# Score tiles computed once, and zero matmuls in the steps of a transformer kernel that have no side work

## The chip, the cores and the metric

The kernel runs on one core of a Trainium2 chip. Its engines work side by side and wait for each other by semaphores: TensorE (PE; its weight loads are shown apart as PEld) multiplies matrices into PSUM, ScalarE (ACT) and VectorE (DVE) read PSUM and write SBUF, GpSimd (POOL) does small things and issues some DMAs, SyncE (SP) issues the other DMAs. The metric is the device time of one execution in microseconds, the median of several.

## The reference

Two layers, each an attention block and a token mixer, over 2048 tokens of width 640, with 32 heads of width 20. Matrix inputs are bf16.

```python
def _A_ref(x, wqkv, wo):                       # x: [1, 2048, 640], H = 32, Dh = 20
    q, k, v = split_heads(x @ wqkv)
    scores = jnp.einsum("bhqd,bhkd->bhqk", q, k) * (Dh ** -0.5)
    p = _softmax(scores, axis=-1)
    o = jnp.einsum("bhqk,bhkd->bhqd", p, v)
    return merge_heads(o) @ wo

def _B_ref(x, w1, b1, w2, b2):                 # mixes along the 2048 tokens, F = 1536
    h = _layernorm(x, axis=-1)
    u = _gelu(jnp.einsum("bsd,sf->bdf", h, w1) + b1)
    y = jnp.einsum("bdf,fs->bds", u, w2) + b2
    return y.transpose(0, 2, 1)

x = x + _A_ref(_layernorm(x), A_wqkv, A_wo)    # twice, with the same weights
x = x + _B_ref(_layernorm(x), B_w1, B_b1, B_w2, B_b2)
```

The softmax is over 2048 x 2048 scores per head, so each attention takes 134 million exponentials.

## The kernel before

**Stages.** A start (layer norm, transposition, V and the first K and Q projections), attention 0, the mixer's two matmul stages with the next layer's start folded into the second, attention 1, the mixer again. The change lies inside `attention`, which runs twice, and in the constants made at the kernel's beginning.

**Units, chunks and tiles.** An attention has 4 query blocks of 512, 8 groups of 4 heads and 16 key tiles of 128, which is 512 units `(qb, g, kt)` in this order. Each unit has four chunks, one a head, of 128 keys x 512 queries, in the order of `HORDER = (0, 2, 1, 3)`. Chunks are taken three at a time, so that one score tile `S` has 128 x 1536 numbers in three PSUM banks; there are 683 tiles per attention (the last has two chunks) and two buffers for them. A score matmul (`s_matmul`, L320) uses 64 rows of the array; heads 0 and 1 of a group lie in the lower 64 rows and heads 2 and 3 in the upper 64, and two neighbours are told apart by a masked copy of the queries (`qev`, `qod`). `HORDER` alternates between the halves.

**A step.** The loop over `t` at the end of `attention` writes out, for each step: the scores of tile `t + 1` (`emit_S`), the exponential of tile `t` on ScalarE into a bf16 tile `P` (`emit_exp`, L348), the PV matmuls of a unit if the exponentials they need are at least one step old (`emit_PV`, L546), and fill (`emit_fills`). PV has four matmuls per unit, one a head, each with 32 columns (20 of V, one of ones that sums the denominators, padding), placed at the columns 0, 32, 64 and 96 of the array, all into the four quarters of one accumulator tile `acc`. It stays open over the 16 key tiles of a group; `start` is set at the first, and after the last `normalize` takes it out of `acc_tiles` and VectorE transposes and divides it (L357 to L364). There is one buffer for it. As 4 chunks make a unit and 3 a tile, three steps of four have a PV and one has none.

**Fill.** Other TensorE work is cut into groups in `fill_queue`: the K and Q projections of later groups and query blocks (L227), the output projection (L448, L481), and the first part of the mixer's first matmul (L421), whose sums go through `ustg` to DRAM by POOL's DMA queue. `emit_fills` takes up to `FILL_NOPV = 3.0` units of cost in a step without PV and `FILL_PV = 1.5` in one with, and pauses one step after each finished group. `planned_fill` says ahead of a step if it will have fill.

**The repeat.** In a step without fill, `emit_S` is given `reps = R_DEFAULT = 1` and writes the same score matmuls of tile `t + 1` a second time. The results are the same.

**Order.** All TensorE instructions are chained in the order in which they are written out (`pe`). The order of the other engines' instructions is found by a scheduler from the dependences. On POOL the kernel's beginning has the identity's memset (masks.py), `warm` (L98, L99), two bias loads (L118, L119, issued as DMAs) and the layer norm's `rstd` (L169); SP issues the loads of x (L776, L786) and of the weights.

Of the kernel before, what the change touches and what calls it, by code (L numbers as in the profile page):

```python
# [11 lines left out]
BF16 = mybir.dt.bfloat16  # L12
# [12 lines left out]
VW = 24  # L25

CFG = dict(
    R_DEFAULT=1,
    FILL_NOPV=3.0,
    FILL_PV=1.5,  # L30
    PV_LAGT=1,
# [8 lines left out]
def kernel(  # L40
# [12 lines left out]
    nc = tc.nc  # L53
# [11 lines left out]
    def pe(inst):  # L65
        tc.chain_iter_dep("pe_order", inst.ins)
        return inst
# [12 lines left out]
    consts = ctx.enter_context(tc.tile_pool(name="consts", bufs=1))  # L80
# [16 lines left out]
    warm = consts.tile([128, 1], F32, name="warm")  # L97
    nc.gpsimd.tensor_tensor(out=warm[:], in0=mhalf[:], in1=mhalf[:], op=ALU.mult)  # L98
    nc.gpsimd.tensor_tensor(out=warm[:], in0=warm[:], in1=mhalf[:], op=ALU.pow)  # L99
    x1lp = ctx.enter_context(tc.tile_pool(name="x1lp", bufs=1))  # L100
    x1last = x1lp.tile([128, 4, D], F32, name="x1last")
    hhp = ctx.enter_context(tc.tile_pool(name="hhp", bufs=1))
# [141 lines left out]
    def attention(st, x_in_ap, x_mid, uacc_l):  # L244
        layer = st.layer
        KT, hT = st.KT, st.hT
        with ExitStack() as p1:
# [18 lines left out]
            S_tiles, P_tiles, acc_tiles, qm_tiles, attnT_tiles = {}, {}, {}, {}, {}  # L266
# [21 lines left out]
            def on_unit_start(n):  # L288
                qb_n, g_n, kt_n = units[n]
                fill_state["unit"] = n  # L290
                if qb_n == 0 and kt_n == 0:
                    if g_n + KQA < NG:
                        enqueue_kq_for_group(g_n + KQA)
                    if g_n == max(0, NG - KQA) and NQB > 1:
                        enqueue_qproj(1)
                if qb_n >= 1 and g_n == 0 and kt_n == 2 and qb_n + 1 < NQB:
                    enqueue_qproj(qb_n + 1)
                if not proj_enqueue_done[0]:
                    last_k_block = max(0, NG - 1 - KQA)
                    if NQB == 1:  # L300
                        done = (qb_n == 0 and g_n >= last_k_block)
                    elif NQB == 2:
                        done = (qb_n == 0 and g_n >= max(0, NG - KQA)) or qb_n >= 1
                    else:
                        done = (qb_n == NQB - 2 and (g_n > 0 or kt_n >= 2)) or qb_n > NQB - 2
                    proj_enqueue_done[0] = done
                check_hT_dead()
                if kt_n == 0:
                    ensure_ready(qb_n, g_n)
                    prep_block(qb_n, g_n)  # L310
                if kt_n == NKT // 2 and n + NKT < NU:
                    nqb, ng, _ = units[n + NKT - kt_n]
                    if ("Q", nqb, ng) not in pending_keys():
                        prep_block(nqb, ng)

            def s_matmul(St, slot, n, j):
                qb, g, kt = units[n]
                jj = j // 2
                q = qm_tiles[(qb, g)][j % 2]
                pe(nc.tensor.matmul(St[:, slot, :], lhsT=KT[64 * jj:64 * jj + 64, g, kt * 128:(kt + 1) * 128],  # L320
                                    rhs=q[64 * jj:64 * jj + 64, :], start=True, stop=True,
                                    tile_position=(64 * jj, 0)))

            def emit_S(t, reps):
                cs = chunks[3 * t:3 * t + 3]
                for (n, j) in cs:
                    if j == HORDER[0]:
                        on_unit_start(n)
                St = sps.tile([128, 3, 512], F32, name="S")
                S_tiles[t] = St  # L330
                for _rep in range(reps + 1):
                    i = 0
                    while i < len(cs):
                        n, j = cs[i]
                        if i + 1 < len(cs) and cs[i + 1][0] == n and (j, cs[i + 1][1]) in ((0, 2), (1, 3)):
                            s_matmul(St, i, n, j)
                            s_matmul(St, i + 1, n, cs[i + 1][1])
                            i += 2
                        else:
                            s_matmul(St, i, n, j)  # L340
                            i += 1

            def emit_exp(t):
                St = S_tiles.pop(t)
                ncs = len(chunks[3 * t:3 * t + 3])
                P = ptp.tile([128, 3, 512], BF16, name="P")
                P_tiles[t] = P
                nc.scalar.activation(out=P[:, 0:ncs, :].rearrange("p a b -> p (a b)"),  # L348
                                     in_=St[:, 0:ncs, :].rearrange("p a b -> p (a b)"),
                                     func=ACT.Exp, scale=SCALE)  # L350
# [186 lines left out]
            def emit_PV(n):  # L537
                qb, g, kt = units[n]
                if kt == 0:
                    acc_tiles[(qb, g)] = accp.tile([128, 512], F32, name="acc")  # L540
                acc = acc_tiles[(qb, g)]
                for j in range(4):
                    ci = 4 * n + HORDER.index(j)
                    P = P_tiles[ci // 3]
                    hh = 4 * g + j
                    pe(nc.tensor.matmul(acc[32 * j:32 * j + 32, :],  # L546
                                        lhsT=Vaug[:, (kt * H + hh) * VW:(kt * H + hh) * VW + 32],
                                        rhs=P[:, ci % 3, :], start=(kt == 0), stop=(kt == NKT - 1),
                                        tile_position=(0, 32 * j)))
                for t_ in list(P_tiles.keys()):  # L550
                    if (3 * t_ + 2) // 4 <= n:
                        del P_tiles[t_]
                if kt == NKT - 1:
                    normalize(qb, g, acc_tiles.pop((qb, g)))
                    if qb == LASTQB and PARTIAL_LAST:
                        if g % 2 == 1:
                            enqueue_outproj_partial(qb, g)
                    elif g == NG - 1:
                        enqueue_outproj(qb)

            def emit_fills(budget, pool_alloc):
                fs = fill_state
                if fs["cooldown"] > 0:
                    fs["cooldown"] -= 1
                    return 0.0
                spent = 0.0
                while spent < budget:
                    if fs["cur"] is None:
                        if not fill_queue:
                            break  # L570
                        if fill_queue[0].get("not_before", 0) > fs["unit"] and budget < 100:
                            break
                        fs["cur"] = fill_queue.popleft()
                        fs["idx"] = 0
                        fs["tile"] = pool_alloc()
                    grp = fs["cur"]
                    grp["mms"][fs["idx"]](fs["tile"])
                    spent += grp["cost"][fs["idx"]]
                    fs["idx"] += 1
                    if fs["idx"] == len(grp["mms"]):  # L580
                        grp["evac"](fs["tile"])
                        fs["cur"] = None
                        fs["cooldown"] = CFG["FILL_GAP"]
                        break
                return spent
# [4 lines left out]
            def planned_fill():  # L590
                if fill_state["cooldown"] != 0:
                    return False
                if fill_state["cur"] is not None:
                    return True
                return len(fill_queue) > 0 and fill_queue[0].get("not_before", 0) <= fill_state["unit"]

            LAGT = CFG["PV_LAGT"]
            pv_done = 0
            emit_S(0, 0)
            for t in range(NTILES):  # L600
                has_fill = planned_fill()
                reps = 0 if has_fill else CFG["R_DEFAULT"]
                if t + 1 < NTILES:
                    emit_S(t + 1, reps)
                emit_exp(t)
                n_pv = 0
                while pv_done < NU and (4 * pv_done + 3) // 3 <= t - LAGT:
                    emit_PV(pv_done)
                    pv_done += 1
                    n_pv += 1  # L610
                emit_fills(CFG["FILL_PV"] if n_pv else CFG["FILL_NOPV"], misc_alloc)
            in_attention[0] = False
            while pv_done < NU:
# [149 lines left out]
    with ExitStack() as a_stack:  # L763
        st0 = open_a_scope(0, a_stack)
        with ExitStack() as p0:
# [29 lines left out]
            setup_wo()  # L795
            setup_biases()
        attention(st0, A_x[0], xd[0], uacc[0])
    with ExitStack() as a_stack:
        st1 = open_a_scope(1, a_stack)
# [59 lines left out]
```

## Time and profile before

| | |
|---|---|
| median of 3 runs | 2105.06 us (2104.55 to 2106.12) |
| the profiled execution's own time | 2106.7 us |
| its span | 2104.9 us |
| TensorE busy | 1953.5 us, 93%, 13278 matmuls |
| ScalarE busy | 1931.5 us, 92%, 1504 instructions |
| VectorE busy | 570.0 us, 27% |
| POOL busy | 148.2 us, 7% |
| exponentials (L348) | 1366, 1839.9 us busy, 1500 ns mean |
| score matmuls (L320) | 6014 |
| PV matmuls (L546) | 4096 |

How it is read: one execution is recorded by the profiler. Busy time counts an engine's own instructions; the mean of one can be longer than its share, since neighbours overlap. A group's row gives, after the counts, the busy time, the mean of one in ns, and the idle time of the engine just before these instructions with what ended most of it. The chain of waits is the work that ended last, followed back from the end: from each piece to what released it. The timeline merges neighbouring instructions of one kind (x8: eight of them); its first number is the start and its second the time that they took, in us, and a bracket gives the idle time before. A row of the windows view gives, for a stretch of time, its length and the busy time and count of PE, PEld, DVE, ACT and POOL, then the granted clock of TensorE (1.00 is full), the share of the DMA engines, and GB/s.

### The profile page before, as it was taken

The numbers are of one execution on the slowest core, as the hardware profiler recorded it, in microseconds if no ns is written. First come the engines' busy times: TensorE is split into PE (matmuls) and PEld (weight loads), VectorE is DVE, ScalarE is ACT, GpSimd is POOL, SyncE is SP. The second block draws the span as 40 slices with busy tenths as digits, with TensorE's granted clock in tenths as the row PEclk, the third lists the DMA queues.
The fourth block names the chain that finished last, engine by engine and source line by source line (L and its number), as shares of the span: only waits on it lengthen the run. The fifth ranks groups of instructions, "written<-read, shape, count | busy, mean of one in ns | idle before, by whom it ended". The sixth has DMA issues, their size and how long they took to land.

```text
span 2104.9 us, 31825 instructions
## 1 busy us (share of the span) xinstructions
PE 1953.5 (93%) x13278; PEld 657.3 (31%) x13278; DVE 570.0 (27%) x1231; ACT 1931.5 (92%) x1504; POOL 148.2 (7%) x218
## 2 busy tenths in 40 slices
PE   7999999999999999997999999999999999999979
PEld 4222222233223332223542222222332233222335
DVE  6122222221322132223642122322113220322242
ACT  5999999999999999996349999999999999999952
POOL 2000000110012001110000000001100120011000
PEclk9999999999999999998999999999999999999989
DMA  5000000110034012223620000001101340222245
GB/s 129 1 1 1 1 18 22 61 53 10 29 58 71 1 35 44 37 26 118 211 81 1 1 1 1 26 28 65 47 14 38 66 63 1 57 49 36 38 121 182
DMA packets 90737, 96.88 MB, mean 46 GB/s; under 512 B 9696, under 2 KB 68192, under 8 KB 90592
## 3 DMA queue, kind: packets, MB, share of 16 engines
q1 hardware_dynamic: 70464, 71.22, 11.0%
q0 software_dynamic: 20128, 23.62, 7.5%
q8 instruction: 104, 1.70, 0.3%
q14 instruction: 41, 0.34, 0.1%
HBM read 55.48 MB, written 39.32 MB: 45 GB/s over the span
## 4 chain that ended last, share of the span: by engine, by line
ACT 58%; PE 25%; issue 13%; DVE 3%; DMA 1%; POOL 0%; SPq 0%; DVEq 0%; ACTq 0%; POOLq 0%
ACT P L348 58%; PE S L320 10%; PE y L741 4%; PE acc L546 3%; PE misc L227 3%; PE pp L218 2%; PE big L670 1%; PE misc L448 1%; DMA ua<-uacc 1%; PE pp L227 0%; DVE T L357 0%; PE S L481 0%; DMA x0in<-in_A_x_dram 0%; DVE bnst L158 0%; PE misc L481 0%
## 5 line engine op out<-in xcount | busy, mean ns | idle before, releaser
L348 ACT ACTIVATE P<-S 128x1536 bf16<-128x1536 f32 (+1 forms) x1366 | 1839.9, 1500 | 8.3 <-PE S L320 7.0
L320 PE MATMUL S<-qev,KT 64*128 64x512 bf16 x2962 | 836.8, 377 | 96.2 <-ACT P L348 90.1
L320 PE MATMUL S<-qod,KT 64*128 64x512 bf16 x3052 | 838.2, 379 | 9.1 <-ACT P L348 4.6
L320 PEld LDWEIGHTS <-KT 64*128 64x128 bf16 x6014 | 326.7, 93 | 655.5 <-issue 486.4
L546 PE MATMUL acc<-P,Vaug 128*32 128x512 bf16 x4096 | 409.9, 389 | 6.2 <-DVE T L357 4.3
L546 PEld LDWEIGHTS <-Vaug 128*32 128x32 bf16 x4096 | 106.5, 92 | 439.0 <-issue 439.0
L427 DVE COPY ustg<-misc 128x512 f32<-128x512 f32 (+1 forms) x144 | 70.0, 486 | 296.6 <-PE misc L421 296.5
L169 POOL TENSOR_TENSOR rstd<-veps,mhalf 128x1 f32<-128x1 f32 x64 | 35.5, 554 | 1187.6 <-DVE veps L164 1068.4
L432 POOL DMA_DIRECT2D uacc<-ustg x96 | 83.0, 864 | 473.6 <-DVE ustg L427 444.3
L421 PE MATMUL misc<-h2st,w1st 128*128 128x512 bf16 (+1 forms) x576 | 115.8, 303 | 0.0
L741 PE MATMUL y<-uT,w2s 128*128 128x512 bf16 (+1 forms) x768 | 107.8, 299 | 3.4 <-ACT uT L684 3.4
L508 DVE CAST QTq<-misc 128x512 bf16<-128x512 f32 x62 | 42.8, 691 | 214.2 <-PE misc L227 214.2
L227 PE MATMUL misc<-hh,wq_pad 128*128 128x512 bf16 x310 | 98.9, 385 | 0.0
L357 DVE STREAM_TRANSPOSE T<-acc 128x512 f32<-128x512 f32 x64 | 45.9, 717 | 186.4 <-PE acc L546 186.4
L508 DVE CAST KT<-misc 128x512 bf16<-128x512 f32 x56 | 38.7, 691 | 212.9 <-PE misc L227 212.9
L227 PE MATMUL misc<-hh,wk_pad 128*128 128x512 bf16 x280 | 87.2, 385 | 0.0
L279 DVE TENSOR_SCALAR qev<-QTq,mask_ev 128x512 bf16<-128x512 bf16 x64 | 22.6, 353 | 235.4 <-PE S L320 234.8
L448 PE MATMUL misc<-wo_pad,attnT 128*128 128x512 bf16 (+1 forms) x384 | 76.8, 303 | 0.0
L741 PEld LDWEIGHTS <-w2s 128*128 128x128 bf16 x768 | 59.6, 98 | 49.9 <-issue 5.0
L76 ACT CAST Vaug<-pp 128x500 bf16<-128x500 f32 (+1 forms) x32 | 14.3, 453 | 52.5 <-PE pp L218 52.5
L457 DVE TENSOR_TENSOR x1s<-misc,xin 128x512 f32<-128x512 f32 (+1 forms) x48 | 23.5, 489 | 131.5 <-PE misc L448 131.5
L218 PE MATMUL pp<-wv,hh 128*128 128x500 bf16 (+1 forms) x320 | 52.0, 313 | 1.7 <-DVE hh L78 1.5
(77 smaller groups left out, 715.9 us busy)
## 6 DMA issues: line engine op xcount, KB each, us to landing
uacc<-ustg POOLq DMA_DIRECT2D x72, 256.0 KB, 4.0
w2s<-in_B_w_dram SPq DMA_DIRECT2D x16, 768.0 KB
w1st<-in_B_w_dram SPq DMA_DIRECT2D x36, 256.0 KB
xd<-x1s SPq DMA_DIRECT2D x24, 320.0 KB
x1in<-xd SPq DMA_DIRECT2D x24, 320.0 KB
ua<-uacc SPq DMA_DIRECT2D x24, 320.0 KB
xd<-x2s SPq DMA_DIRECT2D x16, 320.0 KB
xin<-xd SPq DMA_DIRECT2D x16, 320.0 KB
```

The source lines that it names most:

```text
L218: pe(nc.tensor.matmul(pp[:, 0:c1 - c0], lhsT=st.hT[:, dt_, tt * 128:(tt + 1) * 128], rhs=wv[:, dt_, c0:c1], start=(dt_ == 0), stop=(dt_ == ...
L227: pe(nc.tensor.matmul(t[:, :], lhsT=wpad[:, dt_, g, :], rhs=st.hT[:, dt_, tb * 512:(tb + 1) * 512], start=(dt_ == 0), stop=(dt_ == NDT - 1)))
L320: pe(nc.tensor.matmul(St[:, slot, :], lhsT=KT[64 * jj:64 * jj + 64, g, kt * 128:(kt + 1) * 128], rhs=q[64 * jj:64 * jj + 64, :], start=Tru ...
L348: nc.scalar.activation(out=P[:, 0:ncs, :].rearrange("p a b -> p (a b)"), in_=St[:, 0:ncs, :].rearrange("p a b -> p (a b)"), func=ACT.Exp, ...
L357: nc.vector.transpose(out=T1[:], in_=acc[:])
L421: pe(nc.tensor.matmul(t[:, 0:w], lhsT=states[fp]["w"][:, sti, ftl * 128:(ftl + 1) * 128], rhs=tiles4[sti][:, c0:c1], start=(sti == 0), sto ...
L427: nc.vector.tensor_copy(out=stg[:, 0:w], in_=t[:, 0:w])
L432: nc.gpsimd.dma_start(out=dst, in_=stg[:, 0:w], accum_op=ALU.add)
L448: pe(nc.tensor.matmul(t[:, 0:w], lhsT=attnT[:, g, ttl * 128:(ttl + 1) * 128], rhs=wo_pad[:, g, c0:c1], start=(g == 0), stop=(g == NG - 1)))
L508: nc.vector.tensor_copy(out=dst_ap, in_=t[:, :])
L546: pe(nc.tensor.matmul(acc[32 * j:32 * j + 32, :], lhsT=Vaug[:, (kt * H + hh) * VW:(kt * H + hh) * VW + 32], rhs=P[:, ci % 3, :], start=(kt ...
L741: pe(nc.tensor.matmul(y[:, 0:w], lhsT=w2s[:, ft, sl * 128:(sl + 1) * 128], rhs=uT[:, ft, c0:c1], start=(ft == 0), stop=(ft == NF - 1)))
```

## The change

It takes away the repeat: `emit_S` loses its argument and writes each score matmul once. It adds `keep_busy`: in a step without fill, after the PV and ahead of `emit_fills`, it writes sets of four matmuls with 32 columns each, at the columns 0, 32, 64 and 96, onto the accumulator that is open (`start=False`, `stop=False`). Their weights `zw` are zeros and their moving operand `zr` is ones, 128 x 512, so that they add zero. The number of sets is `SLOTS - 2 - n_pv` with `SLOTS = 4`: one with a PV in the step, two without. If no accumulator is open, none is written. `zw` and `zr` are two new constants, set by POOL at the kernel's beginning.

```diff
 CFG = dict(
-    R_DEFAULT=1,
+    SLOTS=4,
     FILL_NOPV=3.0,
...
     nc.gpsimd.tensor_tensor(out=warm[:], in0=warm[:], in1=mhalf[:], op=ALU.pow)
+    zw = consts.tile([128, 32], BF16, name="zw")
+    nc.gpsimd.memset(zw[:], 0.0)
+    zr = consts.tile([128, 512], BF16, name="zr")
+    nc.gpsimd.memset(zr[:], 1.0)
...
-            def emit_S(t, reps):
+            def emit_S(t):
                 cs = chunks[3 * t:3 * t + 3]
...
-                for _rep in range(reps + 1):
-                    i = 0
-                    while i < len(cs):
-                        n, j = cs[i]
-                        if i + 1 < len(cs) and cs[i + 1][0] == n and (j, cs[i + 1][1]) in ((0, 2), (1, 3)):
-                            s_matmul(St, i, n, j)
-                            s_matmul(St, i + 1, n, cs[i + 1][1])
-                            i += 2
-                        else:
-                            s_matmul(St, i, n, j)
-                            i += 1
+                for i, (n, j) in enumerate(cs):
+                    s_matmul(St, i, n, j)
+
+            def keep_busy(count):
+                for acc in acc_tiles.values():
+                    for _ in range(count):
+                        for j in range(4):
+                            pe(nc.tensor.matmul(acc[32 * j:32 * j + 32, :], lhsT=zw[:], rhs=zr[:], start=False,
+                                                stop=False, skip_group_check=True, tile_position=(0, 32 * j)))
...
-            emit_S(0, 0)
+            emit_S(0)
             for t in range(NTILES):
                 has_fill = planned_fill()
-                reps = 0 if has_fill else CFG["R_DEFAULT"]
                 if t + 1 < NTILES:
-                    emit_S(t + 1, reps)
+                    emit_S(t + 1)
                 emit_exp(t)
                 n_pv = 0
                 while pv_done < NU and (4 * pv_done + 3) // 3 <= t - LAGT:
                     emit_PV(pv_done)
                     pv_done += 1
                     n_pv += 1
+                if not has_fill:
+                    keep_busy(CFG["SLOTS"] - 2 - n_pv)
                 emit_fills(CFG["FILL_PV"] if n_pv else CFG["FILL_NOPV"], misc_alloc)
```

## The prediction

> **What bounds the kernel now.** I read the page first (busy shares, chain, costliest groups), then ScalarE's rows of the timeline across both attentions, then the chain of waits and the timeline inside single steps, last the windows with the granted clock.
>
> ```profile
> span 2104.9 us, 31825 instructions
> PE 1953.5 (93%) x13278; PEld 657.3 (31%) x13278; DVE 570.0 (27%) x1231; ACT 1931.5 (92%) x1504; POOL 148.2 (7%) x218
> L348 ACT ACTIVATE P<-S 128x1536 bf16<-128x1536 f32 (+1 forms) x1366 | 1839.9, 1500 | 8.3 <-PE S L320 7.0
> L320 PE MATMUL S<-qev,KT 64*128 64x512 bf16 x2962 | 836.8, 377 | 96.2 <-ACT P L348 90.1
> L320 PE MATMUL S<-qod,KT 64*128 64x512 bf16 x3052 | 838.2, 379 | 9.1 <-ACT P L348 4.6
> L546 PE MATMUL acc<-P,Vaug 128*32 128x512 bf16 x4096 | 409.9, 389 | 6.2 <-DVE T L357 4.3
> ```
>
> Two engines are nearly full. 1366 exponentials are 1840 of 2105 us, and ScalarE idles before them for 8.3 us in all. TensorE runs 6014 score matmuls (L320) where 2 x 2048 = 4096 would do: 1918 are repeats. How far is ScalarE from its own limit? Its timeline, merged where it never pauses, with the first and the last exponential of each attention:
>
> ```profile
> 49.79 10.85 ACT L348 ACTIVATE P<-S 128x1536 bf16<-128x1536 f32 x8 [0.72 <-PE S L320]
> ...
> 689.05 51.22 ACT L348 ACTIVATE P<-S 128x1536 bf16<-128x1536 f32 x38
> ...
> 968.72 3.77 ACT L348 ACTIVATE P<-S 128x1536 bf16<-128x1536 f32 x3
> 1093.53 2.79 ACT L348 ACTIVATE P<-S 128x1536 bf16<-128x1536 f32 x2 [0.73 <-PE S L320]
> ...
> 2012.47 5.12 ACT L348 ACTIVATE P<-S 128x1536 bf16<-128x1536 f32 x4
> ```
>
> An undisturbed run of 38 gives (51.22 - 1.515)/37 = 1.3434 us per exponential (1.515 is the median of one; they overlap their neighbours). 683 at that pace need 682 x 1.3434 + 1.5 = 917.7 us. The attentions take 972.49 - 49.79 = 922.7 and 2017.59 - 1093.53 = 924.1 us. So ScalarE loses 5.0 + 6.4 = 11.4 us to late scores. That is the ceiling of any gain here, unless an exponential itself gets faster.
>
> Why are scores late? The chain of waits through four steps has TensorE's prices:
>
> ```profile
> 123.53 1.02 PE S L320 x6
> 124.55 0.33 PE acc L546 x4
> 124.88 0.58 PE S L320 x3
> 125.46 0.33 PE acc L546 x4
> 125.79 0.54 PE misc L227 x2
> 126.33 0.53 PE S L320 x3
> ```
>
> A tile costs 0.53 to 0.58 us once and 1.02 twice, so the repeat is 0.44 to 0.49 (0.22 a slot; three matmuls are two slots, since two of 64 rows run together). Four PV matmuls of 32 columns cost 0.33, that is one slot of 0.22 plus 0.11 at the change of shape; their rows begin together (four in 0.40 where one is 0.389). A step without fill with PV costs 1.02 + 0.33 = 1.35 us against ScalarE's 1.343: TensorE has no slack there, and the exponential waits for the repeat too, since that writes the same tile. One stall in full:
>
> ```profile
> 106.51 2.86 ACT L348 ACTIVATE P<-S 128x1536 bf16<-128x1536 f32 x2
> 108.50 0.39 PE L320 MATMUL S<-qev,KT 64*128 64x512 bf16 x2
> 109.16 0.38 PE L320 MATMUL S<-qod,KT 64*128 64x512 bf16 x1
> 109.63 1.45 ACT L348 ACTIVATE P<-S 128x1536 bf16<-128x1536 f32 x1 [0.26 <-PE S L320]
> ```
>
> At pace the third exponential would start at 106.51 + 2 x 1.343 = 109.20; it starts at 109.63, after six matmuls (108.50 to 109.54). Three would have been ready by about 109.1: the loss of 0.43 is the repeat.
>
> **The change part by part.** *Repeats removed:* 1918 matmuls in 320 of 683 steps per attention, 0.44 us each time on TensorE and, where TensorE was behind, on ScalarE. *Zero matmuls added:* 702 sets of four in the new instruction list (351 per attention: one set in 248 steps, two in 50, three at the end; 21 steps without fill get none, as no accumulator is open). They stand behind PV and ahead of the fill, so no exponential waits for them, only the next tile's scores do. No row shows a set right behind PV. Lower bound 0.22 (the repeat's slot, same shape in a row), upper bound 0.33 (the whole PV row); I take 0.22, as the nearest row is two stretches of one shape. The step is then 0.54 + 0.33 + 0.22 = 1.09 us, at the upper bound 1.20. Without PV it is 0.54 + 0.33 + 0.22 = 1.09 with two sets, at most 1.20. All are under 1.343. What hides the sets is that slack; past 0.47 a set (0.35 without PV) it is gone.
>
> *Steps with fill* are unchanged: 0.54 + 0.33 + 0.54 = 1.41 us with two wide fills, over ScalarE's pace by 0.07. Two in a row lose 0.14, which the second score buffer absorbs, and the cycle of four steps above falls from 5.07 to 4.85 of 5.37 us. Fill order, PV order and the waits for DVE's transposition of the accumulator (4.3 us in 16 times) stay; a zero set never follows a unit's last PV. So scores are ready ahead of ScalarE nearly everywhere: -11.4 us, with -7 as the weak end if a third of the stalls have another cause.
>
> *Start:* two memsets on POOL (128x128 takes 0.20; 128x512 is at most four times that) fall in the first 3 us, ahead of the first rstd at 6.96. The scheduler also moves the first bias load's issue (1.21 us) from before the first rstd to behind the third, next to the other (1.36), so the fourth rstd goes from 13.25 to about 14.6; queued behind it are the other rstds, and DVE's fourth h_bf waits for it. TensorE wants that tile only after 17.10 + 1.98 = 19.1, so I cost it 0, bounds 0 and +1.3. On SP one x load passes one wo load: 0, bounds -0.4 and 0 (an issue is 0.4).
>
> *The clock.* Fewer slots per step could let it fall. What the trace shows of that, per window (PE busy second number, clock behind POOL):
>
> ```profile
> 474.40:477.80 3.40, 3.20 (x25) 1.22 (x25) 0.00 (x0) 3.40 (x4) 0.00 (x0) 1.00 0.00 0
> 970.50:973.92 3.42, 1.83 (x13) 0.39 (x9) 0.90 (x2) 1.99 (x2) 0.00 (x0) 1.00 0.00 0
> 973.92:977.33 3.41, 1.24 (x5) 0.53 (x6) 2.64 (x6) 0.00 (x0) 0.00 (x0) 0.50 0.86 287
> 2014.98:2018.40 3.42, 2.44 (x18) 0.67 (x17) 0.33 (x1) 2.60 (x3) 0.00 (x0) 1.00 0.32 78
> 2018.40:2021.81 3.41, 0.53 (x4) 0.29 (x5) 2.82 (x6) 0.00 (x0) 0.00 (x0) 1.00 1.14 308
> ```
>
> The clock halved after a window 54% busy (970.50), and stayed after one 71% busy (2014.98). A long stretch without fill is 94% busy now (474.40) with about 4.75 slots a step; four slots take 0.75 x 0.22/1.343 = 12 points off: 82%, above the 71% that held. Where a unit's last PV and a step without PV follow each other, sets are missing: 3, 2 and 4 slots, some 1.2 fewer on average, so about 62%, between the two rows. I find such places about three times per attention. I take no dip, and carry it as a rival.
>
> [...]
>
> *Sum:* 2106.7 (profiled execution; its span 2104.9) - 11.4 + 0 = 2095.3. The median of the runs, 2105.06, lies 1.6 under the profiled time, so 2093.7; I say 2094, 0.5% faster. The measurement tells 0.2%, about 4.2 us, from no change.
>
> **The rivals.**
> 1. *Dips at the thin places.* A window of 3.41 us at half clock doubles the slots: 4 x 0.43 + 0.21 = 1.93 us a step, 0.6 over pace, 1.5 us in 2.5 steps. Six places: up to 9 us; 2097 to 2103. For it: 62% lies near 54%. Against: windows must align. 10%.
> 2. *Slower: zero matmuls don't count as activity for the clock.* Then steps without fill look like 2.75 slots on average, in every long stretch without fill (about 155 steps per attention): 94% - 2 x 16 points = about 61% busy. If the clock falls in every other window there, 0.3 us a step x 310 = +93 on the old time: about 2198. It decides if zeros don't count and the limit lies above 61%. Against: no row says that it weighs more than matmuls running. 7%.
> 3. *The four of a set run one after another*, since they add onto one bank: 0.86 instead of 0.22. A step with PV is then 0.54 + 0.33 + 0.86 = 1.73 us, 0.39 over pace, one without 0.54 + 0.11 + 1.72 = 2.37, 1.03 over; three of the one to one of the other make 0.55. The long stretches overrun by 155 x 0.55 = 85, the cycles of four (some 165) by 5.49 - 5.37 = 0.12 each, 20: 105 us per attention, about 2315. Against: PV does the same at one slot. 3%.
> 4. *No effect:* the stalls are ScalarE's own, not the repeat's: 2103 to 2107. Against: the stall at 109.63. 5%.
>
> **How the numbers follow.** Forecast 75%, own range 2090.5 (all stalls and a little of the cold clock between stages) to 2098 (-7). With rival 1 the range 2090.5 to 2102 holds 84%; the rest lies above. Faster by over 0.2% (under 2100.9): 0.75 + 0.07 = 0.82. Same: 0.03 + 0.04 = 0.07. Slower: 0.10 + 0.01 = 0.11.
>
> **What the profile after would show.** L320's successor has 4096 matmuls, zero rows 2808; both attentions near 917.7 us; ScalarE's idle before exponentials under 2 us; TensorE's wait for ScalarE up from 94.7 us to about 180; clock 1.00 throughout the attentions. Wrong would be: windows of 0.50 inside an attention (rivals 1, 2), zero sets over 0.35 apiece (3), or exponentials still late behind three matmuls (4).

## The result and the profile after

| | before | changed |
|---|---|---|
| median, us | 2105.59 (2104.55 to 2107.29, 4 runs) | 2095.35 (2093.53 to 2098.76, 4 runs) |
| ratio, 95% interval | | 0.9954 (0.9942 to 0.9966) |
| profiled execution, us | 2106.7 | 2095.81 |
| span, us | 2104.9 | 2094.0 |
| attention 0 and 1, us | 922.7, 924.1 | 917.4, 919.1 |

The changed kernel is 0.46% faster. From its page, the head and four groups (count, busy time, mean of one in ns, idle before with what ended it):

```profile
span 2094.0 us, 33607 instructions
PE 1847.1 (88%) x14168; PEld 572.8 (27%) x14168; DVE 569.7 (27%) x1231; ACT 1926.5 (92%) x1504; POOL 148.2 (7%) x220
L350 ACT ACTIVATE P<-S 128x1536 bf16<-128x1536 f32 (+1 forms) x1366 | 1835.0, 1772 | 3.0 <-PE S L324 2.9
L324 PE MATMUL S<-qev,KT 64*128 64x512 bf16 x2048 | 591.3, 379 | 143.9 <-ACT P L350 136.3
L324 PE MATMUL S<-qod,KT 64*128 64x512 bf16 x2048 | 590.1, 380 | 59.6 <-ACT P L350 53.7
L342 PE MATMUL acc<-zr,zw 128*32 128x512 bf16 x2808 | 257.6, 382 | 0.0
```

TensorE is 106 us less busy; its wait for ScalarE ahead of scores rose from 94.7 to 190.0 us. ScalarE's idle time before exponentials fell from 8.3 to 3.0 us. One reading traps: the mean of one exponential rose from 1500 to 1772 ns, and yet the engine is faster. With scores ready early each row begins sooner inside its predecessor's time, so the row is longer and the pace the same. The pace is read from first start to last end, as in these rows of ScalarE's timeline:

```profile
48.17 2.79 ACT L350 ACTIVATE P<-S 128x1536 bf16<-128x1536 f32 x2 [0.72 <-PE S L324]
...
958.67 6.89 ACT L350 ACTIVATE P<-S 128x1536 bf16<-128x1536 f32 x5
1087.01 2.79 ACT L350 ACTIVATE P<-S 128x1536 bf16<-128x1536 f32 x2 [0.73 <-PE S L324]
...
1783.41 5.54 ACT L350 ACTIVATE P<-S 128x1536 bf16<-128x1536 f32 x4 [1.21 <-PE S L324]
...
1999.25 6.89 ACT L350 ACTIVATE P<-S 128x1536 bf16<-128x1536 f32 x5
```

Attention 0 takes 965.56 - 48.17 = 917.4 us, attention 1 2006.14 - 1087.01 = 919.1. The first stands at ScalarE's pace (917.7 was worked out before); the second holds a stall of 1.21 us at 1783. Of the 10.9 us by which the span is shorter, 5.3 + 4.9 are the attentions', 1.6 lie ahead of the first exponential (49.79 to 48.17), and the stretches between and behind them are 0.4 and 0.6 longer.

A step without fill in TensorE's timeline, first of the kernel before, then of the changed kernel:

```profile
487.64 0.40 PE L546 MATMUL acc<-P,Vaug 128*32 128x512 bf16 x4
488.03 0.37 PE L320 MATMUL S<-qod,KT 64*128 64x512 bf16 x1
...
488.98 0.40 PE L546 MATMUL acc<-P,Vaug 128*32 128x512 bf16 x4
```

```profile
470.23 0.58 PE L324 MATMUL S<-qod,KT 64*128 64x512 bf16 x2
470.74 0.40 PE L548 MATMUL acc<-P,Vaug 128*32 128x512 bf16 x4
470.97 0.39 PE L342 MATMUL acc<-zr,zw 128*32 128x512 bf16 x4
471.57 0.39 PE L324 MATMUL S<-qev,KT 64*128 64x512 bf16 x2 [0.21 <-ACT P L350]
```

The set of zeros starts 0.23 us behind PV, and now TensorE waits 0.21 us for ScalarE in a step with PV. Before, no bracket stands between one PV and the next, 1.34 us later: it had no pause there. The stall at 1783 and a smaller one of 0.28 us at 1524 follow windows of the clock at 0.50. The windows view of the changed kernel (length, PE busy, further engines, then the clock behind POOL):

```profile
479.30:482.70 3.40, 2.11 (x17) 0.52 (x16) 2.33 (x4) 3.40 (x4) 0.00 (x0) 1.00 0.00 0
1516.92:1520.33 3.41, 2.02 (x15) 0.52 (x13) 2.12 (x4) 3.41 (x4) 0.00 (x0) 1.00 0.02 5
1520.33:1523.75 3.42, 3.42 (x23) 0.53 (x22) 0.25 (x1) 3.42 (x3) 0.00 (x0) 0.50 0.00 0
1523.75:1527.16 3.41, 3.20 (x35) 0.80 (x33) 0.00 (x0) 3.13 (x4) 0.00 (x0) 1.00 0.00 0
```

At two thin places of attention 1 (where a group's last PV and a step without PV follow each other, so that sets are missing) the clock halved for one window (3.41 us from 1520.33 and 3.41 from 1779.74), a dip, after windows in which TensorE was 59% busy (1516.92, and 2.02 of 3.41 us at 1776.33); one of 62% (479.30) held.

### The profile page after: what moved, and what is told of

Same layout as the page of the kernel before. It is cut to its first block, busy times and chain, and to the rows that moved or that the text cites. A ratio compares the mean times of both kernels' runs of the same rounds, so it can differ in the third digit from the quotient of the medians.

```text
span 2094.0 us, 33607 instructions
## 1 busy us (share of the span) xinstructions
PE 1847.1 (88%) x14168; PEld 572.8 (27%) x14168; DVE 569.7 (27%) x1231; ACT 1926.5 (92%) x1504; POOL 148.2 (7%) x220
## 4 chain that ended last, share of the span: by engine, by line
ACT 74%; issue 11%; PE 10%; DVE 2%; DMA 1%; POOL 0%; SPq 0%; DVEq 0%; POOLq 0%; ACTq 0%
ACT P L350 74%; PE y L744 5%; PE S L324 1%; PE pp L222 1%; DMA ua<-uacc 1%; PE misc L231 1%; PE acc L548 1%; PE big L673 1%; PE pp L231 0%; DVE utmp L683 0%; PE S L483 0%; DVE bnst L162 0%; POOL rstd L173 0%; DVE x1last L496 0%; PE tp L215 0%
## 5 line engine op out<-in xcount | busy, mean ns | idle before, releaser
L350 ACT ACTIVATE P<-S 128x1536 bf16<-128x1536 f32 (+1 forms) x1366 | 1835.0, 1772 | 3.0 <-PE S L324 2.9
L324 PE MATMUL S<-qev,KT 64*128 64x512 bf16 x2048 | 591.3, 379 | 143.9 <-ACT P L350 136.3
L324 PE MATMUL S<-qod,KT 64*128 64x512 bf16 x2048 | 590.1, 380 | 59.6 <-ACT P L350 53.7
L324 PEld LDWEIGHTS <-KT 64*128 64x128 bf16 x4096 | 221.6, 93 | 687.3 <-issue 659.0
L342 PE MATMUL acc<-zr,zw 128*32 128x512 bf16 x2808 | 257.6, 382 | 0.0
L342 PEld LDWEIGHTS <-zw 128*32 128x32 bf16 x2808 | 64.9, 95 | 43.9 <-issue 43.9
```

The lines of the kernel that those rows point to most:

```text
L342: pe(nc.tensor.matmul(acc[32 * j:32 * j + 32, :], lhsT=zw[:], rhs=zr[:], start=False, stop=False, skip_group_check=True, tile_position=(0, ...
```

## The experiments

Theory A has two halves: the gain comes from the exponential no longer waiting for the repeat that writes its tile, and the zero sets keep the clock up except at the thin places. The rivals: it is TensorE's slack that counts and not the place of the work (B); the sets are not needed (C); a set costs more than its slot. Attention times below are from the first start to the last end of ScalarE's exponentials in each profile. The ratios are to the kernel before as it ran beside each one: a median of 2106.76 us (9 runs), and of 2105.84 us (7 runs) for three and six slots. The profile of the kernel without sets is of its longest run, that of three slots of its shortest.

| kernel | median, us | ratio to before, 95% | attentions, us |
|---|---|---|---|
| no zero sets | 2127.28 | 1.0095 (1.0074 to 1.0117) | 936.2, 934.8 |
| three slots | 2127.23 | 1.0103 (1.0086 to 1.0120) | 926.3, 925.6 |
| four slots, the change again | 2095.94 | 0.9953 (0.9940 to 0.9965) | 917.9, 918.6 |
| four slots, thin places filled | 2094.54 | 0.9946 (0.9934 to 0.9959) | 917.9, 917.8 |
| five slots | 2095.86 | 0.9948 (0.9932 to 0.9963) | 918.4, 917.9 |
| six slots | 2146.32 | 1.0190 (1.0175 to 1.0205) | 943.9, 943.2 |

### The repeats gone and nothing in their place

```diff
-    SLOTS=4,
+    SLOTS=2,
```

> The changed kernel without its zero matmuls (repeats gone, nothing in their place). Theory A, the sets hold the clock: a long stretch without fill then has 3, 3, 3 and 2 slots of 0.22 us a step of 1.343, about 45% of the time in matmuls, where the two dips of the changed kernel came after windows of 43 and 44% and 45% held; so windows of clock 0.50 appear inside both long stretches without fill of each attention, some ten or more, and ScalarE loses there and where fill begins on a cold clock: attentions 919 to 935 us each, total 2097 to 2125. Rival C, the sets are not needed: clock 1.00 in the attentions but for a window or two, 917.5 us each, total 2092 to 2096.

Measured: 2127.28 us (2119.11 to 2132.75), 1% slower than before, a little over the upper end given. The clock line of its page, in 40 slices, and two windows (a long stretch without fill, one with fill):

```profile
PEclk9999899986999589995999999999869985999769
```

```profile
490.00:515.00 25.00, 24.34 (x108) 3.77 (x105) 1.91 (x4) 24.41 (x19) 0.00 (x0) 0.50 0.00 1
300.00:340.00 40.00, 33.90 (x235) 10.72 (x236) 14.13 (x34) 40.00 (x31) 2.20 (x4) 1.00 0.15 47
```

The clock stands at 0.50 through most of the long stretches without fill and at 1.00 in most of those with fill. At 0.50 a step lasts 1.51 us instead of 1.343, as TensorE's timeline shows by the distance of two PVs:

```profile
712.17 0.62 PE L548 MATMUL acc<-P,Vaug 128*32 128x512 bf16 x4
713.68 0.62 PE L548 MATMUL acc<-P,Vaug 128*32 128x512 bf16 x4
```

So the sets are needed (rival C falls), and matmuls with zero weights kept the clock up here: with them the same stretch of the changed kernel (490 to 515 us) ran at 1.00, without them at 0.50. Taking the repeats away alone loses 20 us instead of gaining ten.

### Five slots: the old amount of work in the new place

```diff
-    SLOTS=4,
+    SLOTS=5,
```

> The changed kernel with five slots instead of four: one more zero set in every step without fill, so TensorE's work there is 0.54 + 0.33 + 0.44 = 1.31 us with PV, nearly the 1.35 of the kernel before, and the four-step cycle with fill is back at 5.07 us; only the place differs, behind the exponential's scores instead of ahead of it. Theory A, the repeat made the scores late because the exponential waited for it: the gain stays, attentions 917 to 918.5 us, no window of 0.50 inside them, total 2091 to 2095. Rival B, TensorE's slack is what counts: the stalls come back, attentions 921 to 924 us, total 2099 to 2105.

Measured: 2095.86 us (2094.61 to 2096.64), 0.9 over the upper end, with both attentions at 918.4 us or under and no half-clock window inside them. Its waits view has TensorE as short of slack as it was before the change, its timeline has no pause of TensorE in two steps without fill (473.01 - 470.33 = 2.68 us, twice ScalarE's pace), and its page has ScalarE all but undisturbed:

```profile
PE S L324 <- ACT P L350: 86.3, 211, 0.8
```

```profile
470.33 0.40 PE L548 MATMUL acc<-P,Vaug 128*32 128x512 bf16 x4
470.55 0.60 PE L342 MATMUL acc<-zr,zw 128*32 128x512 bf16 x8
...
471.67 0.83 PE L342 MATMUL acc<-zr,zw 128*32 128x512 bf16 x12
...
473.01 0.40 PE L548 MATMUL acc<-P,Vaug 128*32 128x512 bf16 x4
```

```profile
L350 ACT ACTIVATE P<-S 128x1536 bf16<-128x1536 f32 (+1 forms) x1366 | 1835.5, 1707 | 2.2 <-PE S L324 1.5
```

86.3 us of waiting against 94.6 before in the same view: no more slack, and still nearly all the gain. The amounts are not quite equal: by the prices a step with PV has 1.31 us where it had 1.35, one without 1.31 where it had 1.02, so four steps have 5.24 us against 5.07. TensorE has more to do than before and the stalls stay away, so it is the place of the work that made them (rival B falls): behind the scores, filler delays only the next tile, which has a buffer of its own.

### The thin places filled

```diff
-            def emit_S(t):
+            def emit_S(t, reps=0):
...
-                for i, (n, j) in enumerate(cs):
-                    s_matmul(St, i, n, j)
+                for _rep in range(reps + 1):
+                    for i, (n, j) in enumerate(cs):
+                        s_matmul(St, i, n, j)
...
                 has_fill = planned_fill()
+                due = int(pv_done < NU and (4 * pv_done + 3) // 3 <= t - LAGT)
+                bare = not has_fill and not acc_tiles and not due
                 if t + 1 < NTILES:
-                    emit_S(t + 1)
+                    emit_S(t + 1, 1 if bare else 0)
                 emit_exp(t)
+                early = bool(acc_tiles)
+                if not has_fill and early:
+                    keep_busy(CFG["SLOTS"] - 2 - due)
                 n_pv = 0
...
-                if not has_fill:
+                if not has_fill and not early:
                     keep_busy(CFG["SLOTS"] - 2 - n_pv)
```

> The changed kernel with its thin places filled: the sets go ahead of the PV where an accumulator is open, so that the step of a group's last PV has one too, and the six steps per attention with no accumulator at all write their scores twice. Theory A, the two windows of 0.50 in attention 1 come from the thin places: no window of 0.50 inside an attention, both at 917.4 us, total 2091.5 to 2094.5, runs within 2 us of each other. Rival, dips have another cause or the spread of the runs is not theirs: median within 1 us of the same kernel as changed in this call, runs spread over 4 us or more.

Measured: 2094.54 us (2093.96 to 2096.60), attentions 917.9 and 917.8, no half-clock window in either. The places that were 62%, 59% and 59% busy in the changed kernel (at 479.30, 1516.92 and 1776.33; its attentions begin 1.4 and 2.1 us earlier):

```profile
480.69:484.10 3.41, 2.71 (x26) 0.78 (x26) 2.37 (x4) 3.41 (x4) 0.00 (x0) 1.00 0.02 5
1519.00:1522.41 3.41, 2.67 (x27) 0.81 (x20) 1.55 (x3) 3.41 (x4) 0.00 (x0) 1.00 0.00 0
1778.40:1781.80 3.40, 2.66 (x27) 0.81 (x20) 2.38 (x4) 3.40 (x4) 0.00 (x0) 1.00 0.00 0
```

They are 78 to 79% busy now. The dips are gone from the one execution that was profiled. The runs spread over 2.6 us, more than the 2 expected, against 4.8 of the changed kernel (next section), where the dips are not what made the spread of two executions. The median is 1.4 us lower, but the intervals of the two ratios overlap, so this size isn't settled.

### The change again, for its spread

The kernel is the changed one, with no edit.

> The changed kernel as it is, for its spread and a second trace. Theory A: the number of windows of 0.50 inside the attentions differs from execution to execution (0 to 4), because the windows of the clock's control lie anywhere against the kernel, and each costs 0.5 to 1.5 us: 2093 to 2099, median near 2095. Rival: the same two places dip each time, and the time spread comes from elsewhere.

Measured: 2095.94 us (2095.05 to 2099.87). Two dips again, each after a window 59% busy:

```profile
479.70:483.10 3.40, 2.01 (x20) 0.56 (x13) 1.68 (x4) 3.40 (x4) 0.00 (x0) 1.00 0.00 0
483.10:486.50 3.40, 3.40 (x22) 0.44 (x21) 0.69 (x1) 3.03 (x3) 0.00 (x0) 0.50 0.00 0
1780.20:1783.60 3.40, 2.01 (x20) 0.56 (x17) 2.38 (x4) 3.40 (x4) 0.00 (x0) 1.00 0.00 0
1783.60:1787.00 3.40, 3.07 (x15) 0.46 (x15) 0.00 (x0) 2.59 (x2) 0.00 (x0) 0.50 0.00 0
```

One is at the place that had dipped before (1780 then, 1783 now), the other at one that had held (479 then, 483 now), and the place at 1516 held this time. ScalarE idles 0.37 us behind the dip at 483 and 1.21 behind the one at 1783; attention 0 takes 917.9 us against 917.4, attention 1 918.6 (attentions without a dip take 917.4 to 918.4, so a dip's whole cost is known only roughly). Where the dips fall differs from execution to execution, as expected. In the first trace the clock changes at 1520.33, 1523.74, 1779.74 and 1783.16 us, whole multiples of 3.41 us apart; counted from the first exponential of its own trace, the dip at 483.10 does not lie on these steps (432.87 us behind it here, 1472.16 the one at 1520.33 there). The dips don't make the spread between these two, and there the rival is right: the two attentions add up to 1836.5 us in both, and the 4.1 us between the spans (2094.0 and 2098.1) lie ahead of the first exponential (2.1) and between the attentions (1.9). The record gives the mean granted clock of every run, and longer runs of this kernel have a lower one (0.993 at 2093.53 us, 0.988 at 2098.76), but not where in the run it was lost.

### Six slots

```diff
-    SLOTS=4,
+    SLOTS=6,
```

> The changed kernel with six slots. Theory, a set costs 0.22 us and is hidden only while the step stays under ScalarE's 1.343: a step without fill is then 0.54 + 0.11 + 4 x 0.22 = 1.53 us, 0.19 over, in some 155 steps of the long stretches per attention, +29 us each; the cycles of four with fill, 4.85 + 0.44 = 5.29 of 5.37, still fit or nearly. Attentions 944 to 956 us each, total 2150 to 2172; TensorE waits hardly ever for ScalarE in the long stretches. Rival, a set is cheaper than the row of a lone stretch says, or overlaps the next scores: attentions under 925 us, total under 2110.

Measured: 2146.32 us (2145.46 to 2147.88), attentions 943.9 and 943.2, slightly under both ranges. TensorE's timeline in a long stretch:

```profile
481.15 0.40 PE L548 MATMUL acc<-P,Vaug 128*32 128x512 bf16 x4
481.38 0.82 PE L342 MATMUL acc<-zr,zw 128*32 128x512 bf16 x12
482.66 0.40 PE L548 MATMUL acc<-P,Vaug 128*32 128x512 bf16 x4
```

Three sets take 0.82 us where one takes 0.39, so each further one is 0.215. The step is 482.66 - 481.15 = 1.51 us, against 1.53 by the prices, and TensorE is the bound. The slack for filler is thus two sets in a step with PV and three in one without, as with five slots (1.31 us by the prices), and not one more.

### Three slots

```diff
-    SLOTS=4,
+    SLOTS=3,
```

> The changed kernel with three slots: a set only in steps without fill and without PV; every such step then has three slots, 3 x 0.213 / 1.343 = 48% of the time in matmuls. Theory, the clock falls only after a window under about 45%: the long stretches stay at 1.00, with dips at the thin places and where fill is narrow, some 2 to 6 windows; attentions 917 to 922 us, total 2094 to 2102. Rival, the limit lies above 48%, or the clock weighs columns or zeros: the long stretches go cold as without sets, attentions 930 to 936 us, total 2112 to 2130.

Measured: 2127.23 us; the profiled execution took 2110.6 and the other four 2127.12 to 2129.13. The median lies in the rival's range, the attentions of the profiled execution (926.3 and 925.6) between the two. Its mean granted clock is 0.956, that of the other four 0.927 to 0.936, so they lost more to the clock. The trace has both theories. Stretches of one execution, all of the same kind of step:

```profile
489.00:492.40 3.40, 2.50 (x21) 0.78 (x20) 0.00 (x0) 3.40 (x3) 0.00 (x0) 1.00 0.00 0
710.00:730.00 20.00, 20.00 (x93) 3.17 (x94) 2.37 (x4) 19.18 (x14) 0.00 (x0) 0.50 0.00 0
482.38:485.80 3.42, 3.42 (x17) 0.49 (x16) 0.67 (x1) 3.42 (x3) 0.00 (x0) 0.50 0.00 0
485.80:509.60 23.80, 16.59 (x129) 5.15 (x126) 0.71 (x2) 23.80 (x19) 0.00 (x0) 1.00 0.00 1
687.18:690.60 3.42, 2.14 (x20) 0.73 (x17) 0.00 (x0) 3.42 (x4) 0.00 (x0) 1.00 0.00 0
1758.97:1762.38 3.41, 2.14 (x21) 0.72 (x17) 0.43 (x2) 3.41 (x4) 0.00 (x0) 1.00 0.02 5
```

Three slots kept a full clock at 489 us, 74% busy, and on to 509.60. In the later stretch the clock fell at 704.25 and then stayed at half for 44 us with TensorE busy without a pause; another such stretch from 1526.86 lasted 41 us, and both ended where fill began again. Yet four times (the windows at 475.56, 482.38, 690.60 and 1748.73) a single half-clock window of the same work sufficed. So three slots bring the clock back only sometimes, and the theory missed this. With four slots, one half-clock window sufficed all four times that the two traces show (1520.33 above). Nor does the busy share give a limit for falling: of two windows 63% busy, the one at 687.18 was followed by half clock and the one at 1758.97 was not. Whether the theory's 45% of the time in matmuls is the limit isn't shown.

## Why the prediction was right

*The ceiling, -11.4 us.* Right. The attentions became 10.2 us shorter in the profiled pair, with the dips' cost in them; with the thin places filled they stand at 917.9 and 917.8 us against the 917.7 worked out from an undisturbed run of 38 exponentials. That estimate needed only the pace and two end points, and it bounded everything else.

*The repeat as the cause of the late scores.* Right: with five slots the work is back and the stalls are not. The weak end, -7 if a third of the stalls had another cause, was not needed.

*A zero set costs 0.22.* Right: 0.23 behind PV, 0.215 for each further one. Rival 3 (four one after another) is refuted by that row.

*The start at 0.* The profiled pair has it 1.6 us shorter, but the record shows no effect of the order on POOL or SP. The two memsets took 0.12 and 0.53 us there, the second under four times 0.20. Six more profiles of kernels with the same two memsets have the first exponential at 49.19, 49.87, 49.60, 50.23, 49.66 and 49.51 us, on both sides of the 49.79 before; one of them is of the changed kernel itself, 48.17 in one profile and 50.23 in the other. The x load on the chain takes 5.30 and 7.10 us in these two, and 6.80 before. An effect smaller than this spread can't be told.

*The clock.* "82%" for a long stretch was 81% (8.11 of 10 us at 470 to 480). "I take no dip" is the step that failed: of the six thin places, foreseen at "about 62%" busy between the row that fell at 54% and the row that held at 71%, two dipped in each of the two profiled executions. TensorE's idle times don't tell these from the others: the longest is 0.76 us in the window that fell at 1516.92 and in the one that held at 479.30. The step at half clock, put at 1.93 us, took 1.94 (PV at 1520.34 and at 1522.28). The price of a dip was overstated where 1.5 us was put: ScalarE idled 0.28, 1.21, 0.37 and 1.21 us behind the four, and attention 1, with two of them, took 919.1 us, 1.4 over 917.7. So rival 1 took place in part, next to the forecast rather than instead of it, and 2095.35 lies 1.35 over the 2094 given. Rival 2 (zeros don't count) is refuted by the kernel without sets (0.50 at 490 to 515 us, where the changed kernel has 1.00), rival 4 by the gain. (The totals of rivals 2 and 3 add their loss to the time before, stalls included, and so lie about 11 us too high; nothing here rests on them.)

*The sum.* 2095.3 was forecast for the profiled execution and 2095.81 measured. That they are so close is partly luck: 1.6 us less at the start made up for 1.4 of dips and for 1.0 between and behind the attentions, and the forecast has none of these. The attentions are the part that was reasoned out and came true.

*ScalarE's idle time* before exponentials was foreseen under 2 us and is 3.0: 0.72 + 0.73 before the first one of each attention, which the change doesn't touch, and the rest the dips.

## What to carry to other kernels

Work that only keeps an engine awake belongs behind what the bottleneck waits for: here about the same amount of filler cost some 10 us ahead of the exponential's scores (attentions of 922.7 and 924.1 us) and next to nothing behind them (918.4 and 917.9). When filler is cut, the question is not only whether the clock stays up but whether the remaining work brings it back once it has fallen (here three slots stayed at half clock for 44 us from 704 on, and with four it came back after one window, four times of four); test one step less than you ship. The time to win is read as (count x undisturbed pace) against the time from first start to last end, since overlapping rows hide both stalls and gains (here the mean of one rose from 1500 to 1772 ns while the attentions became shorter).

## What the runs showed of the hardware

- The same steps of three slots ran at 1.00 (486 to 510 us) and at 0.50 for 44 us (704 to 748). At half clock a step with PV and no set takes 1.51 us (712.17 to 713.68, without sets), and with three slots TensorE shows no idle time there (20.00 of 20.00 us at 710). Yet the clock stayed at 0.50, while four other half-clock windows of this work were followed by 1.00.
- The busy share did not tell where the clock falls: in the changed kernel the four windows 59% busy were followed by 0.50 and one 62% busy was not, with three slots windows 63% busy did both, without sets one of 68% fell (2.33 of 3.41 us at 2006.54). These kernels mix matmuls of 64 rows, of 32 columns and of full size, and what the clock follows isn't settled by them.
- Matmuls with zero weights kept the clock up in this kernel: with them the stretch from 490 to 515 us ran at 1.00, without them at 0.50.
- Column-packed sets of four matmuls onto one accumulator follow each other at 0.215 us (three sets in 0.82 us, one in 0.39), not more than the 0.22 of a slot of score matmuls.
